# Where a second MoE's weights are decoded: 1.5 or 1.0 halves per step before, 1 or 1.25 after

## The chip, the cores and the metric

The kernel runs on one core of one Trainium2 chip. The metric is the time of one execution in device microseconds; each number given is the median of several runs, or a single profiled execution where that is said. Five engines work side by side, each with its own queue in program order: TensorE (PE, with its weight loads PEld), VectorE (DVE), ScalarE (ACT), GpSimd (POOL) and SyncE (SP), which issues most transfers.

## The reference

```python
def reference(**kwargs):
    attn_out = _attn_ref(q, k, v, s)             # causal attention, 4 x 8 heads, 576 x 64
    x = attn_out.transpose(0, 2, 1, 3).reshape(2304, 512)
    h = np.maximum(x @ moe_w_in, 0.0)            # first MoE: 512 -> 2048 -> 512
    x = (h * h) @ moe_w_out
    h = x @ moe2_w_in                            # second MoE: 512 -> 2048 -> 512
    return (h * np.cos(h)) @ moe2_w_out
```

All inputs are float32, and the weights of both MoEs arrive as 8-byte words (the host only views pairs of 32-bit words).

## The kernel before

The 2304 tokens go through attention and the first MoE in nine blocks of 256 tokens. While TensorE works on block k of the first MoE, the attention of block k+1 is woven in. The last block, k = 8, has no attention beside it. The second MoE then runs over five blocks: four of 512 tokens and one of 256.

Each matrix product is made of three passes: high part by high part, high by low, low by high (PASSES). Each MoE has 16 chunks f of 128 hidden units. A chunk of the first MoE is g1(k, f), 12 matmuls of 256 columns (L736); gact, three ScalarE operations (L747 to L749); grest, the low part gl on VectorE (L755); and g2(k, f), 12 matmuls (L765), two chunks later. A chunk of the second MoE is m2_g1 (L1010), m2_cos (L1022, L1023, L1024, L1027), m2_mul (L1034, and the cast L1035), m2_rest (L1042) and m2_g2 (L1053), two chunks later again. Each of its g1 and g2 has 12 matmuls of 512 columns in the four large blocks.

The weights of a chunk come in two halves: half 2f is the chunk's w_in, used by g1(f), half 2f+1 its w_out, used by g2(f). The second MoE has 32 halves, numbered 0 to 31 here (32 to 63 in the code). One half is worked in six places:
- w_load, a transfer of 512 KB on SP (L288). The second MoE's halves reuse the buffers of the first MoE's, so moe_slot issues two loads after each g2 of the last block.
- w_clip, one ScalarE operation (L701).
- w_bits, two VectorE operations (L707 and L711).
- w_hi, a ScalarE copy to the high part (L719).
- w_lo, a GpSimd subtraction for the low part (L723).

w_step(n) first flushes what the step before has decoded (w_rest: w_hi and w_lo), and then decodes n halves more with w_bits; these wait in the list wrest until the next w_step or w_need. w_need(j) makes sure that every half below j is decoded and flushed: it decodes missing ones on the spot, one at a time, and flushes.

In the last block, step i of 16 decodes int((i+1) * B8_BITS) - int(i * B8_BITS) halves, with none before step 4 (LOAD_LAG). Two drain steps of one half each (DR_BITS) follow. In the first block of the second MoE, step f first calls w_need, and from f = 2 on (P2_WAIT) it decodes a number set by P2_BITS:

```python
if j == 0:
    w_need(2 * NF + 2 * f + 2)
m2_g1(j, f)
m2_cos(j, f)
if j + 1 < len(blocks):
    ready_y(j + 1, f)
...
m2_rest(*steps2[i - 1])
...
if j == 0:
    f1 = max(0, f - P2_WAIT)
    _weave(w_step(int((f1 + 1) * P2_BITS) - int(f1 * P2_BITS) if f >= P2_WAIT else 0))
    w_ahead()
m2_mul(j, f)
```

m2_g2 of chunk f-2 follows at the end of the step. The order of this code is the order of each engine's queue. ready_y splits the next block's input in steps 3 to 6 and 9 to 12: four times a ScalarE cast (L794) and a GpSimd subtraction (L795) each.

Of the kernel before, what the change touches and what calls it, by code (L numbers as in the profile page):

```python
# [33 lines left out]
def _weave(*chains):  # L34

    chains = [iter(c) for c in chains if c is not None]
    while chains:
        for c in list(chains):
            if next(c, c) is c:
                chains.remove(c)  # L40
# [50 lines left out]

EARLY = 16
START_BITS = 1
B8_BITS = 1.5
P2_BITS = 1
CLIP_AHEAD = 2
B0_BITS = 1.5
LOAD_LAG = 3
# [11 lines left out]
def attention_moe_moe_kernel(  # L110
# [686 lines left out]
    def ready_y(j, f):  # L797

        a, c = divmod(f - 1, 6)
        if a in (0, 1):  # L800
            if c == 0:
                load_y(j, a)
            elif c > 1:
                split_y(j, a, c - 2)
# [115 lines left out]
    def w_step(n):  # L920

        js = list(range(nw[2], min(nw[2] + n, wlim[0])))
        while wrest:
            w_rest(wrest.pop(0))
        if js:
            w_clip_to(js[-1])
            for _ in zip(*[w_bits(j) for j in js]):
                yield
            wrest.extend(js)
            nw[2] += len(js)  # L930

    def w_ahead():
        w_clip_to(nw[2] - 1 + min(CLIP_AHEAD if prog[0] > 4 else min(1, prog[0]), stq[0][1] + (XST if nw[2] + 3 < XST_TO else 0) - len(wrest)))
        w_load_to(nw[2] - 1 + (WAHEAD if prog[0] else 3))
# [23 lines left out]
    for k in range(NB1):  # L958
# [8 lines left out]
        for i in range(J):  # L967
# [6 lines left out]
            if k == NB1 - 1:  # L974
                wlim[0] = 2 * NF + 2 * max(0, i - LOAD_LAG)
                bits = int((i + 1) * B8_BITS) - int(i * B8_BITS)
                ready_y(0, i)
# [86 lines left out]
    for i in range(len(steps2) + G2LAG):  # L1064
# [11 lines left out]
        if new:  # L1076
# [4 lines that stand above are left out]
# [50 lines left out]
```

## Time and profile before

| what | us |
|---|---|
| median of 3 runs | 1073.15 |
| lowest, highest | 1068.69, 1075.8 |
| profiled execution, its own time | 1073.8 |
| span of the profile, first to last instruction | 1072.0 |
| TensorE busy (matmuls) | 1009.2 |
| VectorE busy | 723.7 |
| ScalarE busy | 595.9 |
| GpSimd busy | 333.2 |

The span is what the rows below are measured in; their times count from its start. Busy times of an engine can overlap within it, and an instruction's time holds what it waits for once it has started. The mean granted TensorE clock was 0.995 of full speed (1.00 is 2.4 GHz, 0.50 is 1.2 GHz).

### The profile page before, as it was taken

Reading aid. Unit: us, or ns where it says so; the run is one execution under the profiler, and the core shown is the slowest. Engines: PE = TensorE matmul, PEld = TensorE weight load, DVE = VectorE, ACT = ScalarE, POOL = GpSimd, SP = SyncE. Lnnn points to the kernel's source line nnn. Section 1 sums busy time; section 2 is a strip of 40 time slices with the busy share of each in tenths; the row PEclk is TensorE's granted clock in tenths of the full one; section 3 lists DMA queues with packets and bytes.
Section 4 is the critical chain, followed back from the end, with each engine's and each line's share of the span. In section 5 each row is a group of like instructions: output and inputs, shape, how many; then the busy total and the mean of one; then the engine's idle time right before and its main releaser. Section 6 shows DMA issues by size and latency. Waiting matters only on the chain.

```text
span 1072.0 us, 20129 instructions
## 1 busy us (share of the span) xinstructions
PE 1009.2 (94%) x7216; PEld 896.9 (84%) x7216; DVE 723.7 (68%) x1668; ACT 595.9 (56%) x1416; POOL 333.2 (31%) x458
## 2 busy tenths in 40 slices
PE   1888889899999999999999988999999999999998
PEld 1778888799999988989989987788888888888887
DVE  4979779868877897777988189665444444444454
ACT  2779667556667666665665487554333333333343
POOL 5536435534333363333552065333001010000000
PEclk9999999999999999999999999999999999999999
DMA  7934377665776876466787298000100100010010
GB/s 221 353 114 159 102 160 178 163 155 137 178 167 141 183 170 177 112 135 147 172 201 157 77 365 273 25 20 20 40 20 20 40 20 1 20 40 1 0 41 20
DMA packets 150150, 126.64 MB, mean 118 GB/s; under 512 B 108065, under 2 KB 125041, under 8 KB 150049
## 3 DMA queue, kind: packets, MB, share of 16 engines
q1 hardware_dynamic: 145840, 118.20, 41.8%
q0 software_dynamic: 4192, 7.14, 2.4%
q8 instruction: 57, 0.93, 0.4%
q14 instruction: 45, 0.36, 0.1%
q10 hardware_dynamic: 16, 0.01, 0.0%
HBM read 85.25 MB, written 15.81 MB: 94 GB/s over the span
## 4 chain that ended last, share of the span: by engine, by line
PE 76%; DVE 10%; DMA 5%; issue 4%; ACT 3%; POOL 1%; SPq 0%; DVEq 0%; ACTq 0%; POOLq 0%
PE o L1053 19%; PE hp L1010 18%; PE hps L736 15%; PE y L765 14%; PE pvs L585 4%; PE qkp L490 3%; DMA rw<-in_w_dram 2%; DVE gl L755 2%; DMA vb<-v_d 1%; DMA raw<-in_qk_dram 1%; DVE st L711 1%; DVE st L707 1%; DVE sb L504 1%; PE xps L639 1%; ACT sb L521 1%
## 5 line engine op out<-in xcount | busy, mean ns | idle before, releaser
L736 PE MATMUL hps<-xh,wt 128*128 128x256 f32 x1152 | 240.4, 291 | 6.6 <-ACT g L747 6.5
L765 PE MATMUL y<-gh,wt 128*128 128x256 f32 x1152 | 237.3, 289 | 0.0
L736 PEld LDWEIGHTS hps<-xh,wt 128*128 128x128 f32 x1152 | 190.8, 192 | 10.7 <-ACT g L747 8.5
L1010 PE MATMUL hp<-yh,wt 128*128 128x512 f32 (+1 forms) x640 | 197.3, 374 | 0.0
L765 PEld LDWEIGHTS y<-gh,wt 128*128 128x128 f32 x1152 | 189.3, 191 | 1.9
L1053 PE MATMUL o<-wt,gh 128*128 128x512 f32 x576 | 181.1, 396 | 0.2 <-ACT gh L1035 0.2
L765 PE MATMUL y<-gl,wt 128*128 128x256 f32 x576 | 163.1, 283 | 3.2 <-DVE gl L755 3.2
L736 PE MATMUL hps<-xl,wt 128*128 128x256 f32 x576 | 163.8, 284 | 0.1
L1023 DVE TENSOR_SCALAR kf<-a 128x512 f32<-128x512 f32 (+1 forms) x80 | 32.1, 401 | 189.4 <-ACT a L1022 189.4
L747 ACT ACTIVATE g<-hps 128x256 f32<-128x256 f32 x144 | 55.3, 384 | 152.0 <-PE hps L736 145.8
L1010 PEld LDWEIGHTS hp<-yh,wt 128*128 128x128 f32 x640 | 117.3, 188 | 23.9
L347 POOL TENSOR_TENSOR k<-raw,hi 64x576 fp32r<-64x576 f32 (+3 forms) x80 | 105.1, 1314 | 92.6 <-ACT hi L336 79.9
L1053 PEld LDWEIGHTS o<-wt,gh 128*128 128x128 f32 x576 | 107.4, 189 | 24.7 <-ACT gh L1035 1.0
L1010 PE MATMUL hp<-yl,wt 128*128 128x512 f32 (+1 forms) x320 | 119.5, 373 | 0.0
L795 POOL TENSOR_TENSOR yl<-yr,yh 128x256 fp32r<-128x256 f32 x36 | 31.4, 871 | 282.9 <-ACT yh L794 248.5
L1053 PE MATMUL o<-wt,gl 128*128 128x512 f32 x288 | 113.0, 392 | 1.6 <-DVE gl L1042 1.6
L765 PEld LDWEIGHTS y<-gl,wt 128*128 128x128 f32 x576 | 110.1, 191 | 4.1 <-DVE gl L755 3.6
L736 PEld LDWEIGHTS hps<-xl,wt 128*128 128x128 f32 x576 | 111.0, 193 | 0.6 <-DVE xl L656 0.3
L755 DVE TENSOR_TENSOR gl<-g,gh 128x256 fp32r<-128x256 f32 x144 | 94.0, 653 | 17.9 <-PE y L765 13.9
L723 POOL TENSOR_TENSOR wt<-st,wt 128x512 fp32r<-128x512 f32 x56 | 78.9, 1420 | 72.8 <-ACT wt L719 72.7
L1027 ACT ACTIVATE a<-kf 128x512 f32<-128x512 f32 (+1 forms) x80 | 47.2, 590 | 95.1 <-DVE kf L1024 95.0
L521 ACT ACTIVATE sb<-sb,nb 128x128 f32<-128x128 f32 (+8 forms) x160 | 93.8, 586 | 9.0 <-DVE nb L504 8.9
(87 smaller groups left out, 1782.8 us busy)
## 6 DMA issues: line engine op xcount, KB each, us to landing
rw<-in_w_dram SPq DMA_DIRECT2D x64, 512.0 KB
raw<-in_qk_dram SPq DMA_DIRECT2D x32, 352.0 KB
raw<-in_qk_dram SPq DMA_DIRECT2D x16, 384.0 KB
vr<-in_v_dram POOLq DMA_DIRECT2D x16, 320.0 KB, 4.1
v_d<-vt SPq DMA_DIRECT2D x16, 320.0 KB
raw<-in_qk_dram SPq DMA_DIRECT2D x16, 320.0 KB
vb<-v_d SPq DMA_DIRECT2D x32, 160.0 KB
y_d<-yst SPq DMA_DIRECT2D x18, 256.0 KB
```

The lines of the kernel that those rows point to most:

```text
L347: nc.gpsimd.tensor_tensor(out=k2[0:64, BT:BT + nk], in0=raw[0:64, BT:BT + nk], in1=hi[0:64, BT:BT + nk], op=ALU.subtract)
L490: nc.tensor.matmul(p[0:r, 0:cn], m[0:kk, qo:qo + r], m[0:kk, BT + c0:BT + c0 + cn], start=(kk == 128), stop=(kk == 68),)
L521: nc.scalar.activation(out=sb[0:r, 0:w], in_=sb[0:r, 0:w], func=ACTF.Exp, scale=-1.0, bias=j["nb"], accum_out=pd[n - h % 2]["z"][0:r, ti, ...
L585: nc.tensor.matmul(pv[0:r, ti, h % 2, :], pt[0:kr, a * nch + c, :], vb[0:kr, c, m, :], start=(first and c == 0 and a == 0 and m == 0), sto ...
L723: nc.gpsimd.tensor_tensor(out=t[:, 1], in0=wst.pop(j)[1], in1=t[:, 0], op=ALU.subtract)
L736: nc.tensor.matmul(hp, w[:, a, c * 128:(c + 1) * 128], (xh, xl)[e][:, c, :], start=(n == 0), stop=(n == 3 * KD - 1),)
L747: nc.scalar.activation(out=g, in_=hp, func=ACTF.Relu)
L755: nc.vector.tensor_tensor(out=gl, in0=g, in1=gh, op=ALU.subtract)
L765: nc.tensor.matmul(yps[k][d // 2][:, d % 2, :], w[:, a, d * 128:(d + 1) * 128], (gh, gl)[e], start=(f == 0 and n == 0 and d % 2 == 0), sto ...
L1010: nc.tensor.matmul(hp, w[:, a, c * 128:(c + 1) * 128], (yh, yl)[e][:, c, :], start=(m == 0), stop=(m == 3 * KD - 1),)
L1027: nc.scalar.activation(out=a, in_=kf, func=ACTF.Sin, scale=-6.2831850)
L1053: nc.tensor.matmul(ops[j][a], (gh, gl)[e][:, a * 128:(a + 1) * 128], w[:, c, :], start=(f == 0 and m == 0), stop=(f == NF - 1 and m == 2),)
```

## The change

Two constants change. The last block of the first MoE decodes one half of the second MoE's weights in each step instead of one and two by turns, and the first block of the second MoE decodes five halves in four steps instead of four in four.

```diff
-B8_BITS = 1.5
-P2_BITS = 1
+B8_BITS = 1.0
+P2_BITS = 1.25
```

## Rows read from the trace of the kernel before

**Rows 1.** Busy time by stretch: us, PE, PEld, DVE, ACT, POOL, granted clock, DMA share, GB/s.
```profile
627.00:663.00 36.00, 29.68 (x230) 27.94 (x229) 35.83 (x41) 29.05 (x62) 25.85 (x20) 1.00 0.89 317
672.00:674.00 2.00, 0.59 (x3) 0.50 (x4) 1.81 (x4) 0.63 (x1) 0.00 (x0) 1.00 0.04 16
674.00:678.00 4.00, 4.00 (x12) 3.17 (x11) 2.75 (x6) 2.32 (x4) 0.00 (x0) 0.57 0.00 0
678.00:752.00 74.00, 74.00 (x321) 59.84 (x320) 42.42 (x76) 38.43 (x69) 25.20 (x20) 1.00 0.05 15
```
**Rows 2.** Chain of waits in order of time, the first MoE's last block: start, us, what.
```profile
606.62 1.44 PE y L765 x12
608.06 1.44 PE hps L736 x12
...
648.74 1.68 DVE st L711
...
650.45 0.62 ACT wt L719
651.06 0.29 ACT g L747
...
651.40 1.69 PE hps L736 x12
...
664.96 1.67 DVE st L711
```
**Rows 3.** TensorE's waits, 610 to 676 us: who waited for whom, total, times, longest.
```profile
PE hps L736 <- ACT g L747: 4.9, 7, 1.8
PE o L1053 <- DVE gl L1042: 1.6, 1, 1.6
```
**Rows 4.** Groups of instructions, 617 to 673 us: busy us, mean ns of one, idle before.
```profile
L723 POOL TENSOR_TENSOR wt<-st,wt 128x512 fp32r<-128x512 f32 x20 | 28.9, 1460 | 14.3 <-ACT wt L719 14.1
L711 DVE SCALAR_TENSOR_TENSOR st<-rw,st 128x512 int32<-128x512 int32 x20 | 22.8, 1163 | 0.3
...
L707 DVE TENSOR_SCALAR st<-st 128x512 int32<-128x512 int32 x20 | 17.0, 868 | 1.6 <-ACT st L701 1.0 <-DMA rw<-in_w_dram 0.5
...
L755 DVE TENSOR_TENSOR gl<-g,gh 128x256 fp32r<-128x256 f32 x13 | 9.2, 710 | 3.2 <-PE y L765 3.2
...
L795 POOL TENSOR_TENSOR yl<-yr,yh 128x256 fp32r<-128x256 f32 x7 | 6.4, 920 | 7.1 <-ACT yh L794 7.0
```
**Rows 5.** Line 711, 677 to 740 us: shortest, median, longest ns, first and last start.
```profile
L711 DVE SCALAR_TENSOR_TENSOR st<-rw,st x12: 691/692/693, 677.5 to 738.9; 128x512 int32<-128x512 int32 x12
```
**Rows 6.** Chain in order of time, step 12 of the second MoE: start, us, what.
```profile
730.52 2.76 PE o L1053 x12
733.28 2.81 PE hp L1010 x12
```
**Rows 7.** ScalarE in order of time, the same step: start, us, instruction, idle before.
```profile
730.55 0.60 ACT L1022 ACTIVATE a<-hp 128x512 f32<-128x512 f32 x1 [0.87 <-PE hp L1010]
...
733.27 0.62 ACT L719 CAST wt<-st 128x512 fp32r<-128x512 f32 x1
734.64 0.62 ACT L1035 CAST gh<-a 128x512 fp32r<-128x512 f32 x1 [0.75 <-DVE a L1034]
```
**Rows 8.** VectorE in order of time, the same step.
```profile
732.86 0.42 DVE L707 TENSOR_SCALAR st<-st 128x512 int32<-128x512 int32 x1
733.31 0.69 DVE L711 SCALAR_TENSOR_TENSOR st<-rw,st 128x512 int32<-128x512 int32 x1
733.92 0.68 DVE L1034 TENSOR_TENSOR a<-a,hp 128x512 f32<-128x512 f32 x1
```
**Rows 9.** GpSimd in order of time, the same step.
```profile
733.44 1.17 POOL L795 TENSOR_TENSOR yl<-yr,yh 128x256 fp32r<-128x256 f32 x1 [3.15 <-ACT yh L794]
734.57 1.27 POOL L723 TENSOR_TENSOR wt<-st,wt 128x512 fp32r<-128x512 f32 x1
```
**Rows 10.** TensorE in order of time, the last block's longest gap.
```profile
640.08 0.39 PE L736 MATMUL hps<-xh,wt 128*128 128x256 f32 x1 [1.82 <-ACT g L747]
```

## The prediction

> **What bounds the kernel now.** I read the busy time by stretch first, then the chain of waits in order of time, then TensorE's waits, then single engines in order of time. From 678 us on TensorE is the bound: 74.00 us busy of 74.00 [rows 1]. Every idle microsecond put in front of it there lengthens the run, and none can be won there. In the last block of the first MoE it is another engine: between 627 and 663 us VectorE is busy 35.83 of 36 us and TensorE only 29.68, so 6.32 us of TensorE are lost [rows 1]. Before that stretch a step of this block takes one g1 and one g2 of 1.44 us each, so 2.88 us is TensorE's floor [rows 2]. The chain shows how VectorE's load reaches TensorE: the second decode instruction L711 ends, only then can ScalarE copy the high part (L719), the ReLU (L747) of the next chunk stands behind that copy in ScalarE's queue, and g1 waits for the PSUM buffer that this ReLU empties [rows 2]. TensorE's waits name the same line: 4.9 us on L747, then 1.6 us on L1042 where the second MoE begins [rows 3].
>
> **What is moved.** I counted the halves from the two formulas. Before: steps 4 to 15 of the last block decode 1, 2, 1, 2, ..., 18 in all, the two drain steps 1 each, and the second MoE's first block one in each step f = 2 to 13 (halves 20 to 31). After: 12 + 2 = 14 in the first MoE, and in the second half 14 at f = 2, 15 at 3, 16 at 4, 17 and 18 at 5, 19 at 6, 20 at 7, 21 at 8, 22 and 23 at 9, 24 at 10, 25 at 11, 26 at 12, 28 and 29 at 13, 30 at 14. Half 27 (at 13) and half 31 (at 15) are then still missing when step f asks for halves up to 2f+1, so w_need decodes them in line. No instruction is added or removed: six halves, each a clip, two VectorE operations, a copy and a GpSimd subtraction, change place. Their DMAs don't move: w_load is issued from moe_slot after each g2 in both kernels, so SP's queue keeps its order.
>
> **The gain in the last block.** With contention in them, one half costs VectorE 1163 + 868 ns there and one gl 710 ns [rows 4]. At 1.5 halves a step this is 1.5 x 2.03 + 0.71 = 3.76 us; the stretch holds 230 matmuls, 9.6 steps of 24, which is 3.76 us a step [rows 1]. The model fits. At one half it is 2.74 us, below TensorE's 2.88. So most of the 6.32 us come back; I leave 1.0 for uneven steps, since the margin is 0.14 us a step: **-5.3** (bounds -2.7 and -6.3). What is late next is TensorE itself. L711 at 664.96 takes 1.67 us against 0.692 alone [rows 2, 5] and stands ahead of the first chunk of the second MoE; with less GpSimd work queued there I take **-0.5** (0 to -1.6, the whole wait on L1042 [rows 3]).
>
> L711 takes 692 ns wherever no subtraction runs beside it and up to a mean of 1163 where they do [rows 4, 5]. The Trainium skill ("SBUF — State Buffer", Who interferes with whom) says that VectorE with two SBUF inputs and GpSimd shut each other out for a whole instruction. Taken literally, 1.5 halves would cost 1.5 x (1.11 + 1.46) us plus 0.61 for eight y splits in 12 steps, 4.47 us a step without gl; the trace has 3.76, so it is not that strict here. By the rule the gain would be about 2.7 us instead of 5.3, and the sum +18.1.
>
> **The price in the second MoE: deadlines.** Step f runs g1(f), then g2(f-2). Call T the end of g1(f-1). g1(f) would start at T + 2.76, and needs the high part of half 2f at once, and its low part from the third matmul (0.47 us later: two of twelve in 2.81), at T + 3.23. Step 12 of before shows when a flush is done; T is 730.52 and g1(13) starts at 733.28 [rows 6]. The first activation starts at 730.55, the copy L719 at 733.27, the cast L1035 runs 734.64 to 735.26 [rows 7]; the low part runs on GpSimd behind a y split, 734.57 to 735.84, that is T + 5.32 [rows 9]. In the kernel before this is no wait: it is half 29, not needed by g1(13). The latest g1 half there, 30, is decoded at f = 12 and flushed at 13, a whole step early. After the change the halves of g1(11) to g1(15) come late:
> f = 11: half 22, decoded at 9, flushed inside step 10: ready at T + 5.32 plus 0.05 for the signal (651.35 to 651.40 [rows 2]), 2.1 after T + 3.23. Step 9 has two decodes; the second adds 0.45 + 0.61 us to VectorE [rows 8], which pushes the cast at its end past the next step's first activation by 0.2 to 1.1; I take 0.6. Sum 2.7.
> f = 12: half 24, decoded at 10, flushed inside step 11: 2.1.
> f = 13: half 26, decoded at 12, flushed only by w_need ahead of g1(13). Its copy stands on ScalarE behind the cast L1035 of step 12, T + 4.74; then 0.6 copy, 0.05, 1.3 subtraction: T + 6.7, 3.45 late.
> f = 14: half 28, one of two decoded at 13, so 1.0 later still: 4.45.
> f = 15: half 30, like 13: 3.45.
> Together **+16.2** (15.7 with 0.2 for step 9; 18.5 if TensorE waits for the low part already at the first matmul, 0.47 x 5). Nothing covers these waits: everything behind g1 in TensorE's order waits too, and each deadline counts from the end of the g1 before, so an early stall buys no time for the next half. The second halves of each pair go to g2, two steps later, and are in time. Steps f = 5, 6 and 9 with more work on VectorE only eat its idle time.
>
> **The clock.** After the idle time at 672 to 674 us (0.59 busy) TensorE was granted 0.57 from 674 to 678, half speed for most of it, which costs 4 x 0.43 = 1.7 us [rows 1]. It isn't certain: after 1.82 us of idle time at 640.08 us [rows 10] the stretch from 627 to 663 kept 1.00 [rows 1]. The five stalls are longer than either. Bounds 0 and 5 x 1.7 = 8.5; I take three falls, **+5.1**.
>
> **Sum.** -5.3 - 0.5 + 16.2 + 5.1 = +15.5 us. The profiled execution took 1073.8 us (span 1072.0), 0.65 above the median of the three runs, so 1089.3 on its scale and 1088.6 on the median's; I give 1088.5.
>
> **Rivals.** (A) The stalls come, the clock doesn't fall: +10.4, some 1083.5, down to 1081 with the whole gain. For it: the gap at 640 us. Against: the stalls repeat in every step. Chance 0.27.
> (B) VectorE and GpSimd serialise, so that the last block stays behind them (L707 and L711 alone 0.42 + 0.69 [rows 8], L723 1.46, eight y splits of 0.92 over 12 steps 0.61 [rows 4]: 3.18 us a step even without gl, above 2.88), and all five stalls drop the clock: 16.2 + 8.5 - 0.5 - (0 to 2.7), +21.5 to +24, 1095 to 1097. The Trainium skill's page on SBUF, named above, would have it so. Against: the fit of 3.76 us. Chance 0.12.
> (C) Faster: the flushes are in time. This decides at T + 3.23: if ScalarE and GpSimd finish a half of the next step there instead of at T + 5.32, because the two engines have idle time in these steps, no stall remains and the last block's gain stands alone, -5.8 to -8, 1065 to 1067. Against it stand the order of the queues and the times of step 12. Chance 0.06.
> (D) Only the three halves flushed by w_need are late (11.35) and the clock holds: +5.6, 1079. Chance 0.05.
> The forecast itself, 1084 to 1095: 0.50.
>
> **How the numbers follow.** The range 1078 to 1095 leaves out C, half of B and the edge of D. About 1%, 10.7 us, is what a measurement here can tell from no change: bounds 1062.4 and 1083.9. Slower by more: nearly all of the forecast, B, and a third of A, 0.68. Within: the rest of A, D, half of C, 0.29. Faster: 0.03.
>
> **What would show it.** Right: in the last block TensorE near 3.0 us a step and VectorE no longer full; in the second MoE's first block five gaps ahead of g1's third matmul, at f = 11 to 15, released by GpSimd's L723 (or ScalarE's L719), of 2 to 4.5 us, and clock rows near 0.5 behind some; everything after that block unchanged. It would be wrong if TensorE's waits there named another line, if the gaps shrank from one to the next, or if the last block still ran at 3.5 us a step.

## The result, and the profile after

The change makes the kernel slower: 1087.3 us (median of 4 runs, 1084.84 to 1088.34) against 1071.8 (4 runs, one more than the table in front has), ratio 1.0137, 95% interval 1.0113 to 1.0160. The profiled execution took 1087.59 us, its span is 1085.8: 13.8 more than the span of before. The forecast was +15.5 us and 1088.5.

The place where the second MoE begins (the first L1010) splits the difference. It lies at 662.3 us in the trace of before and at 654.0 after: 8.3 us won in front of it. From there to the end it is 409.7 us before and 431.8 after: 22.1 lost.

First the busy time by stretch of the changed kernel: us, PE, PEld, DVE, ACT, POOL, granted clock, DMA share, GB/s.

```profile
627.00:654.00 27.00, 27.00 (x227) 26.94 (x226) 20.50 (x28) 22.72 (x52) 18.24 (x14) 1.00 1.02 394
654.00:710.00 56.00, 54.47 (x236) 43.70 (x235) 39.71 (x62) 31.51 (x58) 19.07 (x15) 1.00 0.20 71
710.00:762.00 52.00, 37.41 (x121) 26.69 (x120) 19.93 (x37) 19.74 (x36) 16.00 (x13) 0.84 0.03 11
762.00:836.00 74.00, 74.00 (x320) 59.89 (x319) 33.94 (x57) 27.70 (x50) 5.17 (x7) 1.00 0.06 22
```

The last block of the first MoE is now TensorE's from end to end (27.00 of 27.00), and VectorE has a quarter of its time free, where it was full before [rows 1]. All the loss sits in one stretch, 710 to 762 us: TensorE is idle for 14.59 us of it, and the clock granted in it is 0.84. Behind it nothing has changed: from the second block of the second MoE to the end it is 322.2 us in both traces. The last block, from its first L736 to the second MoE, took 57.3 us before and 49.1 after. The chain of waits in order of time (start, us, what) shows the block at its floor of two times 1.44 us a step up to its end:

```profile
626.67 1.44 PE y L765 x12
628.11 1.44 PE hps L736 x12
...
648.38 1.44 PE hps L736 x12
649.82 4.32 PE y L765 x36
654.14 2.81 PE hp L1010 x12
```

The groups of instructions between 617 and 656 us (busy us, mean ns of one, idle before) show what one half costs VectorE now that fewer subtractions run beside it: 1005 + 608 ns against 1163 + 868 [rows 4].

```profile
L711 DVE SCALAR_TENSOR_TENSOR st<-rw,st 128x512 int32<-128x512 int32 x13 | 13.1, 1005 | 0.4
L707 DVE TENSOR_SCALAR st<-st 128x512 int32<-128x512 int32 x14 | 8.5, 608 | 0.7 <-DMA rw<-in_w_dram 0.5 <-ACT st L701 0.3
```

TensorE's waits from 600 to 800 us (who waited for whom: total, times, longest) name the two flush lines, where before they named L747 [rows 3] and, for 1.5 us, the low part on VectorE, L755. The wait on L1042 is in both.

```profile
PE hp L1010 <- ACT wt L719: 11.2, 5, 3.4
PE hp L1010 <- POOL wt L723: 3.2, 4, 1.2
PE o L1053 <- DVE gl L1042: 1.5, 1, 1.5
```

The line on L755, before, in the view of [rows 3]:

```profile
PE y L765 <- DVE gl L755: 1.5, 1, 1.5
```

Step 12 and the g1 behind it, the same place as [rows 6 to 9], in order of time (start, us, instruction, idle before). ScalarE:

```profile
727.93 0.60 ACT L1022 ACTIVATE a<-hp 128x512 f32<-128x512 f32 x1 [2.74 <-PE hp L1010]
...
732.01 0.62 ACT L1035 CAST gh<-a 128x512 fp32r<-128x512 f32 x1 [0.69 <-DVE a L1034]
732.54 0.61 ACT L719 CAST wt<-st 128x512 fp32r<-128x512 f32 x1
```

GpSimd:

```profile
733.23 2.51 POOL L723 TENSOR_TENSOR wt<-st,wt 128x512 fp32r<-128x512 f32 x2 [1.26 <-ACT wt L719]
```

TensorE:

```profile
733.21 0.75 PE L1010 MATMUL hp<-yh,wt 128*128 128x512 f32 x1 [2.55 <-ACT wt L719]
733.75 0.63 PE L1010 MATMUL hp<-yl,wt 128*128 128x512 f32 x1
734.56 1.22 PE L1010 MATMUL hp<-yh,wt 128*128 128x512 f32 x2 [0.18 <-POOL wt L723]
```

g1(12) ends at 727.90, which is T in this step. The cast L1035 ends 4.74 us later, the copy of half 26 stands behind it, and the third matmul of g1(13), the first that needs the low part, starts at T + 6.67. The first two matmuls already run when only the high part is there; they take 0.75 and 0.63 us instead of 0.40, since the clock has fallen by then. The stretches with a lowered clock (columns as above):

```profile
716.00:720.00 4.00, 4.00 (x12) 3.11 (x12) 0.00 (x0) 0.03 (x1) 0.98 (x1) 0.57 0.01 4
732.00:738.00 6.00, 4.61 (x13) 3.24 (x14) 1.01 (x2) 2.22 (x4) 2.51 (x2) 0.72 0.26 87
742.00:752.00 10.00, 7.62 (x20) 5.62 (x21) 2.08 (x5) 2.25 (x4) 2.51 (x2) 0.66 0.00 1
756.00:762.00 6.00, 5.38 (x17) 4.06 (x16) 0.29 (x1) 0.64 (x2) 2.08 (x2) 0.72 0.01 1
```

Four falls to half speed, the third twice as long as the others: 4 x 0.43 + 6 x 0.28 + 10 x 0.34 + 6 x 0.28 = 8.5 us of full speed, five times the 1.7 of [rows 1].

### The profile page after: what moved, and what is told of

Its sections match the earlier page's. It is cut to its first block, busy times and chain, and to the rows that moved or that the text cites. A ratio compares the mean times of both kernels' runs of the same rounds, so it can differ in the third digit from the quotient of the medians.

```text
span 1085.8 us, 20129 instructions
## 1 busy us (share of the span) xinstructions
PE 1016.3 (94%) x7216; PEld 900.5 (83%) x7216; DVE 716.3 (66%) x1668; ACT 594.9 (55%) x1416; POOL 331.9 (31%) x458
## 4 chain that ended last, share of the span: by engine, by line
PE 75%; DVE 8%; issue 6%; DMA 6%; ACT 3%; POOL 2%; SPq 1%; POOLq 0%; DVEq 0%; ACTq 0%
PE hps L736 17%; PE hp L1010 16%; PE y L765 16%; PE o L1053 16%; PE pvs L585 4%; PE qkp L490 4%; DMA rw<-in_w_dram 2%; DMA vb<-v_d 2%; DMA early<-in_qk_dram 2%; DVE gl L755 1%; POOL wt L723 1%; PE xps L639 1%; DVE sb L504 1%; DVE st L711 1%; DVE hi L344 1%
## 5 line engine op out<-in xcount | busy, mean ns | idle before, releaser
L736 PE MATMUL hps<-xh,wt 128*128 128x256 f32 x1152 | 240.1, 291 | 0.0
L1010 PE MATMUL hp<-yh,wt 128*128 128x512 f32 (+1 forms) x640 | 203.4, 384 | 14.6 <-ACT wt L719 11.2
L736 PEld LDWEIGHTS hps<-xh,wt 128*128 128x128 f32 x1152 | 191.2, 193 | 2.6 <-ACT g L747 0.3
L1023 DVE TENSOR_SCALAR kf<-a 128x512 f32<-128x512 f32 (+1 forms) x80 | 33.0, 413 | 203.2 <-ACT a L1022 203.2
L736 PE MATMUL hps<-xl,wt 128*128 128x256 f32 x576 | 163.9, 285 | 0.1
L1010 PEld LDWEIGHTS hp<-yh,wt 128*128 128x128 f32 x640 | 119.8, 193 | 43.5 <-ACT wt L719 13.3
L747 ACT ACTIVATE g<-hps 128x256 f32<-128x256 f32 x144 | 55.1, 382 | 154.0 <-PE hps L736 148.3
L1010 PE MATMUL hp<-yl,wt 128*128 128x512 f32 (+1 forms) x320 | 122.2, 382 | 0.0
L736 PEld LDWEIGHTS hps<-xl,wt 128*128 128x128 f32 x576 | 111.2, 193 | 0.6 <-DVE xl L656 0.3
L755 DVE TENSOR_TENSOR gl<-g,gh 128x256 fp32r<-128x256 f32 x144 | 92.9, 646 | 25.1 <-PE y L765 16.8
L1022 ACT ACTIVATE a<-hp 128x512 f32<-128x512 f32 (+1 forms) x80 | 44.4, 555 | 108.7 <-PE hp L1010 108.6
```

What stands on the lines that cost most here:

```text
L736: nc.tensor.matmul(hp, w[:, a, c * 128:(c + 1) * 128], (xh, xl)[e][:, c, :], start=(n == 0), stop=(n == 3 * KD - 1),)
L747: nc.scalar.activation(out=g, in_=hp, func=ACTF.Relu)
L755: nc.vector.tensor_tensor(out=gl, in0=g, in1=gh, op=ALU.subtract)
L1010: nc.tensor.matmul(hp, w[:, a, c * 128:(c + 1) * 128], (yh, yl)[e][:, c, :], start=(m == 0), stop=(m == 3 * KD - 1),)
L1022: nc.scalar.activation(out=a, in_=hp, func=ACTF.Copy, scale=1.0 / (2.0 * math.pi), bias=0.25)
```

## The experiments

The theory: a half that reaches the second MoE late is flushed behind ScalarE's and GpSimd's work of the step before, and g1 waits for it (deadlines). The rival: steps that decode two halves overload VectorE and GpSimd there (load). All eight runs in one table. "Falls" are stretches of half speed (one of double length counts twice), in front of the start of the second MoE and behind it. Those in front come in the attention stage, at varying places, but for one of e1's two, which lies in the last block; they move the start of the second MoE, so the length of the last block, from its first L736 to the second MoE, stands beside it. Spans and falls are those of the profiled execution. Each ratio is against runs of the kernel before taken together with that run (their medians are 1071.8 for the change, 1073.4 for e1, e3, e4 and e5, and 1071.8 for e2, e6, e7 and e8).

| run | halves a step: last block, second MoE, from f | median us | ratio to before, 95% | start of second MoE | length of last block | from there to the end | falls in front, behind |
|---|---|---|---|---|---|---|---|
| before | 1.5, 1, 2 | 1071.8 | | 662.3 | 57.3 | 409.7 | 2, 1 |
| the change | 1.0, 1.25, 2 | 1087.3 | 1.0137 (1.0113 to 1.0160) | 654.0 | 49.1 | 431.8 | 2, 5 |
| e1_second_only | 1.5, 1.25, 2 | 1071.5 | 0.9989 (0.9968 to 1.0010) | 661.1 | 57.3 | 409.7 | 2, 1 |
| e2_first_only | 1.0, 1, 2 | 1095.5 | 1.0209 (1.0180 to 1.0238) | 657.4 | 49.0 | 436.0 | 4, 6 |
| e3_in_time | 1.0, 1.5, 1 | 1071.1 | 0.9982 (0.9960 to 1.0004) | 651.8 | 49.0 | 414.8 | 1, 0 |
| e4_flush_now | 1.0, 1.25, 2 | 1077.4 | 1.0041 (1.0018 to 1.0063) | 654.5 | 49.0 | 419.7 | 2, 3 |
| e5_fill | 1.0, 1.25, 2 | 1084.8 | 1.0102 (1.0070 to 1.0134) | 657.8 | 49.0 | 425.8 | 4, 0 |
| e6_from_step0 | 1.0, 1.25, 0 | 1068.0 | 0.9951 (0.9932 to 0.9969) | 656.0 | 49.0 | 410.3 | 3, 0 |
| e7_from_step0_flush_now | 1.0, 1.25, 0 | 1067.2 | 0.9940 (0.9920 to 0.9960) | 656.1 | 49.2 | 410.2 | 2, 1 |
| e8_1125_from_step0 | 1.125, 1.25, 0 | 1065.1 | 0.9940 (0.9917 to 0.9962) | 657.7 | 49.7 | 407.7 | 4, 0 |

**The second constant alone (e1).**

```diff
 B8_BITS = 1.5
-P2_BITS = 1
+P2_BITS = 1.25
```

> Only the second MoE's constant changes (1.5 and 1.25): 20 halves are ready at its start, as in the kernel before, and f = 5 and 9 decode two. Deadline theory: half 30 is decoded at f = 10, every flush is at least a step early, TensorE has no wait in the second MoE's first block, and the time is that of before, within 2 us. Load theory (the steps with two decodes overload VectorE and GpSimd in the second MoE): those steps are here too, so part of the 24 us lost there returns, 5 us or more slower than before.

Measured: no change, and no wait on a flush line. Busy time by stretch, then VectorE in order of time in a step with two decodes:

```profile
678.00:752.00 74.00, 74.00 (x320) 59.84 (x320) 46.71 (x74) 37.62 (x70) 24.84 (x20) 1.00 0.05 15
```

```profile
692.63 0.76 DVE L707 TENSOR_SCALAR st<-st 128x512 int32<-128x512 int32 x2
693.30 2.94 DVE L711 SCALAR_TENSOR_TENSOR st<-rw,st 128x512 int32<-128x512 int32 x2
```

Two L711 take 2.94 us there instead of twice 0.69, beside GpSimd's y split and low part, and still TensorE has not one idle moment in 74 us. At 1.25 a step the load theory falls.

**The first constant alone (e2).**

```diff
-B8_BITS = 1.5
+B8_BITS = 1.0
 P2_BITS = 1
```

> Only the last block's constant changes (1.0 and 1): 14 halves are ready at the second MoE's start, and with one a step half 20 is flushed inside step 9, 22 to 30 only by w_need. Deadline theory: one stall more than in the changed kernel, at f = 10 (some 2 to 3 us) and those at f = 11 and 12 as long as the ones of w_need (2.7 to 3.4), six clock falls of 1.7: 1090 to 1097. Load theory: no step decodes two on its own, so the second MoE runs as before and the last block's 8 us stand: 1065.

Measured: 1095.5, in the range of the deadline theory; the load theory's 1065 is 30 us away. TensorE's waits in the second MoE's first block:

```profile
PE hp L1010 <- ACT wt L719: 12.7, 6, 2.6
PE hp L1010 <- POOL wt L723: 4.2, 6, 1.2
```

Six stalls, from f = 10 on. So the change's second constant takes back some 8 us of what its first one costs, by the medians of different runs.

**The same decodes, flushed earlier (e4).** In the changed kernel:

```diff
                 _weave(w_step(int((f1 + 1) * P2_BITS) - int(f1 * P2_BITS) if f >= P2_WAIT else 0))
+                while wrest:
+                    w_rest(wrest.pop(0))
                 w_ahead()
```

> The changed kernel, but each half is flushed at the end of the step that decoded it; the decodes per step are the same. Deadline theory: halves 22 and 24 come in time (no wait at f = 11 and 12); 26, 28 and 30 are ready at about T + 5.4 to 5.9, so f = 13, 14 and 15 wait some 2.1, 2.6 and 2.1 us instead of 2.7, 3.4 and 3.1. With zero to three clock falls of 1.7 us: 1069 to 1075, 12 or more faster than the changed kernel. Load theory: the work per step is the same, so 1087.

Measured: 1077.4, above the range given and 10 us below the changed kernel, where 12 or more were expected. The waits:

```profile
PE hp L1010 <- ACT wt L719: 4.2, 3, 1.9
PE hp L1010 <- POOL wt L723: 2.0, 3, 0.7
```

Three stalls instead of five, those of halves 26, 28 and 30, 2.56, 1.58 and 2.12 us of idle time. Measured from the end of the g1 before, the third matmul of g1 starts 2.97, 2.70 and 2.54 us later than without a wait, 8.2 together where 6.8 were forecast, and three fall lengths came where none to three were allowed. The decodes of every step are the same as in the changed kernel; only the place of the flush in the queues differs, and the waits of halves 22 and 24 are gone. The other three go in e7 below, where the steps with two decodes remain. Together with e1 that settles it for deadlines and against load.

**The waits filled with matmuls (e5).** In the changed kernel, ahead of g1 of steps 11 to 15 of the first block; the tile written is started anew by g1:

```diff
+        if j == 0 and f >= 11:
+            for x in range(8):
+                nc.tensor.matmul(hp, wt[1, f - 1, 0][:, 0, 0:128], yh[:, x % KD, :], start=True, stop=True)
```

> The changed kernel with eight more matmuls of 0.235 us, 1.9 us, ahead of g1 in steps f = 11 to 15; they write the PSUM tile that g1 then starts anew, and only keep TensorE busy while it would wait. If the four clock falls behind the stalls come from the idle time, they go: the deadlines stay, g1 ends as late in each step, and the time falls by about 8.5 us, to 1079 (6 to 7 slower than before). If the falls cost nothing beside the stalls or come for another reason, the time stays at 1087, or grows by up to 9 us.

Measured: 1084.8, where 1079 was expected. The falls in the second MoE are gone, all of them, though idle time of 0.3 to 2.1 us a step remains, and the third matmul of each g1 starts as late as in the changed kernel (6.85, 5.39, 6.66, 7.47 and 6.67 us after the end of the g1 before). Busy time by stretch and waits:

```profile
712.00:761.00 49.00, 42.53 (x175) 31.75 (x174) 22.87 (x41) 20.13 (x37) 16.63 (x14) 1.00 0.04 12
```

```profile
PE hp L1013 <- POOL wt L723: 3.4, 5, 1.2
PE hp L1013 <- ACT wt L719: 3.1, 4, 1.5
```

With forty matmuls more, the second MoE is 6.0 us shorter than in the changed kernel (425.8 against 431.8). I had expected all 8.5: but part of the lowered clock had run while g1 was waiting anyway, as at 733.21 above, and cost nothing. The median fell by 2.5 us alone. The profiled execution has two falls more in the attention stage than the changed kernel's, and its second MoE starts 3.8 us later; the two medians also come from different sets of runs, and by the two ratios the gain is 0.35%, 3.8 us.

**All halves in time, at 1.5 a step (e3).**

```diff
-P2_BITS = 1.25
+P2_BITS = 1.5
-P2_WAIT = 2
+P2_WAIT = 1
```

> The last block as in the changed kernel (1.0), the second MoE with 1.5 halves a step from f = 1: halves 22 to 30 are decoded three or more steps ahead of their g1. Deadline theory: no waits on L719 or L723 are left, and the gain of the last block stands alone: 8 us there and up to 2 at the second MoE's start, 1061 to 1066, 8 to 10 faster than before. Load theory: more steps with two decodes than in the changed kernel (six against three), so as slow as that or slower, 1087 or more.

Measured: 1071.1, between the two: the deadline theory gave 1061 to 1066. No wait on a flush line and no fall in the second MoE, but another wait has taken their place. TensorE's waits from 670 to 770 us, and VectorE in order of time around step 4:

```profile
PE o L1053 <- DVE gl L1042: 5.0, 5, 1.2
```

```profile
676.47 1.38 DVE L1023 TENSOR_SCALAR kf<-a 128x512 f32<-128x512 f32 x1 [1.41 <-ACT a L1022]
...
679.76 2.94 DVE L711 SCALAR_TENSOR_TENSOR st<-rw,st 128x512 int32<-128x512 int32 x2
682.62 0.67 DVE L1034 TENSOR_TENSOR a<-a,hp 128x512 f32<-128x512 f32 x1
```

With two decodes in every other step, the two low parts of one step run over the cosine of the next (L1023 takes 1.38 us instead of 0.43), two L711 follow with 2.94, and TensorE waits 1.2 us for the low part gl in four steps and 0.2 in a fifth. So the load theory was wrong for the change, but at 1.5 a step load is the next bound.

**In time at 1.25 a step (e6, e7, e8).** Decoding begins at f = 0; e7 has the flush of e4 as well, e8 decodes 1.125 in the last block.

```diff
-P2_WAIT = 2
+P2_WAIT = 0
```

> The changed kernel with decoding from f = 0 instead of f = 2 (1.0 and 1.25). Deadline theory: halves 22 to 28 get a full step between flush and g1; half 30, decoded at 13 and flushed inside 14, is some 1.5 us late. The second MoE's first block costs 0 to 4 us more than its 408 without clock falls, against 423 (falls taken out) in the changed kernel: 1063 to 1068. Load theory: the same two-decode steps, nearly as slow as the changed kernel.

> As the run before, and each half flushed at the end of the step that decoded it. Deadline theory: no half is late, no wait on L719 or L723; the last block's 8 us and up to 2 at the second MoE's start stand alone: 1062 to 1066. If VectorE's load at the second MoE's start (decoding at f = 0 and 1 beside the first cosines) takes the place, the wait on L1042 there grows from 1.5 us.

> 1.125 halves a step in the last block (16 ready at the second MoE's start), 1.25 from f = 0: every half is flushed at least a step early without moving the flush. Deadline theory: no wait on L719 or L723. The last block's VectorE step is 1.125 x 2.03 + 0.71 = 3.0 us against TensorE's 2.88, so 1 to 2 us of its 8 are lost again: 1063 to 1068.

Measured: 1068.0, 1067.2 and 1065.1, each faster than before beyond its interval, e6 by 0.5%, e7 and e8 by 0.6%; e7 lies 1.2 us above the range given. Waits of e6:

```profile
PE o L1053 <- DVE gl L1042: 1.6, 1, 1.6
PE hp L1010 <- ACT wt L719: 1.1, 1, 1.1
PE hp L1010 <- POOL wt L723: 0.8, 1, 0.8
```

One stall of 1.9 us of idle time at f = 15, that of half 30, which was expected late. Waits of e7, no flush line:

```profile
PE o L1053 <- DVE gl L1042: 1.9, 1, 1.9
PE o L1053 <- ACT gh L1035: 0.4, 1, 0.4
```

Its wait at the second MoE's start has grown a little, and a fall of the clock follows it. In e8 only the 1.6 us on L1042 are left, and the second MoE takes 407.7 us. Its last block took 49.7 us against 49.0 with 1.0: 0.7 us lost, where 1 to 2 were expected. e6, e7 and e8 can't be told apart by these runs; any of them beats both kernels.

## Why the prediction was right

The sign, the size and the cause were right: +15.5 forecast, +15.5 by the medians, +13.8 between the two profiled executions. That the sum fits this well is in part luck: the two gains were 4.2 us too small and the two costs 2.5 us too small, and these errors work against each other. The terms, in the two profiled executions:

- **Deadlines, forecast +16.2.** Start of g1's third matmul after T, the end of the g1 before: forecast T + 5.97, 5.37, 6.68, 7.68 and 6.68 for f = 11 to 15; measured 6.87, 5.37, 6.67, 7.48 and 6.66 (715.79, 725.30, 734.56, 745.61 and 756.90, less 708.92, 719.93, 727.90, 738.13 and 750.24). The knock-on of step 9's second decode was too small, 0.6 for 1.5. The due time was too late by 0.16: the chain gives 733.28 for g1(13) [rows 6], which is the end of g2's last record, while TensorE's own records put g1's third matmul of that step at 733.59, T + 3.07 and not T + 3.23. Less 3.07 the five delays are 3.80, 2.30, 3.60, 4.41 and 3.59, together 17.7 (the idle time in TensorE's records is 11.2 + 3.2 = 14.4 there, for a record hides the first part of each gap). That g1 starts as soon as the high part is there, which was left open, holds: in step 13 its first matmul starts before the subtraction has run.
- **Clock, forecast +5.1.** The rest of the second MoE's loss, against 408.0 us for before without its one fall: 431.8 - 408.0 - 17.7 = 6.1. There were five fall lengths, not three, 8.5 us, and part of them was hidden in the waits. The run with filled waits, which has the same five delays and no fall, is 6.0 us shorter.
- **Last block, forecast -5.3.** This was the term that was mis-sized most: -8.3, of which 8.2 in the last block itself, and 8.1 to 8.3 there in all kernels with 1.0. The step is "TensorE only 29.68, so 6.32 us of TensorE are lost", less 1.0 left for uneven steps. The prediction's own step times held the answer: 9.6 steps of 3.76 us against the floor of 2.88 are 8.4. So did the row beside it: weight loads were busy 27.94 of 36 us [rows 1], 8.06 idle. A matmul's record here lasts 0.28 us while starts are 0.12 apart, so it runs on past its slot and hides the first part of a gap behind it. The Trainium skill ("Trainium Kernel Development and Optimization", Performance Expectations) calls matmul busy time a bad metric for how close a kernel is to its roofline, and weight-load busy share a good one; here the two differ by 1.7 us, and the gain of the last block, 57.3 - 49.1 = 8.2, sides with the weight loads. The 1.0 for uneven steps was not needed either: the cost of a half itself fell, with fewer subtractions beside it.
- **Start of the second MoE, forecast -0.5.** The wait on L1042 stayed (1.5 against 1.6 [rows 3]). But the fall of the clock behind it, 1.7 us [rows 1], was there before and is not after. It is missing in six of the seven other runs that decode 1.0 or 1.125 halves in the last block, and present in e1 with 1.5; why was not tried.

TensorE in order of time, first the third matmul of g1(13) before the change, then, after it, those of g1(11), g1(12), g1(14) and g1(15) (that of g1(13), 734.56, stands further above):

```profile
733.59 0.63 PE L1010 MATMUL hp<-yh,wt 128*128 128x512 f32 x2
```

```profile
715.79 0.87 PE L1010 MATMUL hp<-yh,wt 128*128 128x512 f32 x2 [1.22 <-POOL wt L723]
...
725.30 0.73 PE L1010 MATMUL hp<-yh,wt 128*128 128x512 f32 x2 [1.22 <-POOL wt L723]
...
745.61 1.22 PE L1010 MATMUL hp<-yh,wt 128*128 128x512 f32 x2
...
756.90 1.00 PE L1010 MATMUL hp<-yh,wt 128*128 128x512 f32 x2 [0.62 <-POOL wt L723]
```

Against rival A, the clock did fall; against C and D, all five halves were late; against B, the last block ran at TensorE's floor. But that does not show that VectorE and GpSimd run freely side by side, as "not that strict here" in the prediction has it. Single records show the later of two operations longer by nearly what was left of the earlier one. In [rows 8, 9] L711 takes its 0.69 us, and the y split that begins with 0.56 us of it left takes 1.17 instead of its shortest 0.74: 0.43 more. In the changed kernel L711 at 644.60 takes 0.69, and the subtraction that begins with 0.67 us of it left takes 1.83 instead of 1.26: 0.57 more. The shortest, median and longest of the two GpSimd operations before (ns):

```profile
L795 POOL TENSOR_TENSOR yl<-yr,yh x36: 737/743/1192, 614.4 to 967.5; 128x256 fp32r<-128x256 f32 x36
L723 POOL TENSOR_TENSOR wt<-st,wt x56: 1257/1356/1807, 17.2 to 745.1; 128x512 fp32r<-128x512 f32 x56
```

The sums of 4.47 and 3.18 us a step took the means of [rows 4], 1.46 and 0.92, which hold such waits already. With the shortest times B's sum, without gl as it stands there, is 0.42 + 0.69 + 1.26 + 0.49 = 2.86 us, no more than the floor of 2.88; with gl's 0.42 us it is 3.28. So the block at its floor speaks only against an exclusion without any overlap.

With the terms as measured the sum is -8.3 - 1.7 + 17.7 + 6.1 = +13.8.

## What to carry to other kernels

When work is spread differently over steps, list for each piece the step that makes it and the step that needs it, and follow its last operation through each engine's queue: rates that all but cover the need (14 halves ahead and 17 in the steps, for 32) left five of sixteen chunks late, and each lateness counted in full because it was measured from the step before. Give the piece a whole step between flush and use, and the same rates win instead of lose. Matmul records hide the first part of each gap. In the last block weight loads fill TensorE's time when nothing waits (26.94 of 27.00 us), and their idle time gives what can be won. In the second MoE, with 512 columns, they are busy 59.84 of 74.00 us [rows 1] with no wait at all; there, count from the starts of matmuls.

## What the runs showed of the hardware that was not expected

A wait of TensorE does not bring down the clock each time. Behind the five stalls of 1.9 to 3.4 us of idle time in the changed kernel there are four falls, one of them twice as long; behind six in e2 five, one of them twice as long; behind three in e4 two. The single wait at the start of the second MoE, 1.5 to 1.9 us in all ten traces, has a fall behind it in three, before, e1 and e7. The wait of 1.82 us at 640.08 [rows 10] had none; the same wait in e1, 1.83 us at 638.90, had one. Stalls that come in each step are also the longer ones here, and which of the two matters was not tried. Eight matmuls put into each wait removed all falls behind the stalls, which made the second MoE 6.0 us shorter by adding work.

What a fall costs depends on what bounds the stretch: the one in e1's last block (granted clock 0.57 from 639 to 643 us) left the block's length as it was, 57.3 us as in before, where VectorE is the bound. In the attention stage every run has one to four falls, at varying places. The last block starts between 602.8 and 608.8 us in the ten traces; with 1.7 us taken off for each fall in front of it, it is 601.1 to 603.5, so the falls are most of what separates these starts.
